# Moving spectral pieces between the borders of token pairs and the opened steps of a fused Fourier mixing and SiLU kernel

## The chip, the core and the metric

The kernel runs on one core of a Trainium2 chip. The metric is the device time of one execution in microseconds (us). The time before is the median of three runs.

The core's engines work side by side, each through its own instructions in order: PE multiplies matrices and writes to PSUM, a small memory of eight banks; DVE and ACT are the vector and the scalar engine, and both read PSUM; POOL is the third general engine and also issues transfers; SP issues transfers only. A wait on one engine holds all that stands behind it on that engine.

## What is computed

Eight sequences of 3008 tokens with 256 channels are filtered in the frequency domain, and every token then passes through a two-layer network with a SiLU between. All in fp32.

```python
X = np.fft.rfft(x, axis=1)
F = (filt_r + 1j * filt_i)[None, :, :]
y = np.fft.irfft(X * F, n=x.shape[1], axis=1)
...
x = y.reshape(B * S, D)
h = x @ w_in
g = h * (1.0 / (1.0 + np.exp(-h)))
return (g @ w_out).astype(np.float32)
```

## The kernel before

**The token network sets the beat.** The tokens of a sequence are handled in six *token pairs* (two blocks of 256, 256 or 240 tokens, with a fast 2x2 scheme that needs seven products instead of eight). A pair takes eight *steps*, one for each double column block of the weights. A step issues seven full-array matmuls of `hidden` (into the PSUM banks `x` and `yz`) and, between them, seven of `project` for the step before (into the four accumulator banks `a0` to `a3`). A pair ends with its last `project`, which runs between the `hidden` matmuls of the next pair's first step; then `drain` copies the four banks out, and they are free until the next step's `project` opens the new pair's sums. I call that moment, the end of a pair's first step, the *border*. Eight sequences of 48 steps make 384 steps, and their order on each engine is written out by hand: `put(step, rnd, piece)` places a piece of other work behind round `rnd` (0 to 7) of a step.

**The Fourier filter of the next sequence runs in between.** While the network works on sequence b-1, the pieces for sequence b are put among its 48 steps. I number these steps as *places* 0 to 47; the code counts them from the sequence's own start, `at`, so `at - 40` is place 8 of the sequence before, `at + 12` is place 12 of the sequence itself, and `at - 64` is place 32 two sequences ahead. Borders lie at the end of places 0, 8, 16, 24, 32 and 40. For sequences 2 to 7 (sequence 1 has an older form, sequence 0 a prologue) the pieces are:

- *folded stage 1* (`fold`, `stage1_fold`, `evict_fold`, `pairs_fold`), three times (f = 0, 1, 2): DVE folds eight rows of x, PE multiplies into four banks `pf`, ACT copies two of them out, DVE combines these with the other two, and POOL stores eight pieces to DRAM (`d1`);
- *stage 1 of the two middle groups* (`stage1` 6 and 7, `pairs_t1`), banks `pa`;
- *forward* (`forward_two`, g = 0, 2, 4): PE multiplies loaded rows (`load_t2`) into four banks `pb`; `free_two` has ACT copy two of them to SBUF; DVE multiplies all four by the filter (`multiply_two`, four calls of two operations, 128x512 each) and adds (`add_two`);
- *inverse* (`inverse_two`, g = 0, 2, 4): PE fills four banks `pc`; ACT copies two out (`even_two`), DVE combines (`rows_two`, `ends_two`), POOL stores to DRAM (`d2`);
- *last stage* (`stage3`, g = 0 to 7): PE fills two banks `pd` from loaded rows (`load_t4`), and `evict_y` copies one by DVE and one by ACT into the network's input `y`. `stage3` 6 and 7 of a sequence run while the network already works on it.

PE reaches these pieces as blocks of small matmuls (32x32 or 64x64 corners of the array, many side by side).

**Two ways to find banks.** All eight banks are in use in a normal step. At a border the accumulators `a0`..`a3` are free besides the two spare banks `f`, and also `x` and `yz` once the step's last sums are taken: `join` puts `stage3` there, and a step in `joined` starts the new pair with the products for `a0` and `a1`, so that `a2` and `a3` have longer. Elsewhere a step is *opened* (`open_step`, the set `opened`): its first two `project` matmuls run first, then the piece uses `x` and `yz` (`HIDDEN`) and `f`, and only then `hidden` begins.

The places before, for one sequence's pieces within the 48 steps of the network:

```
border  0: stage1_fold 1, stage3 4        opened  4: stage1 6, 7
border  8: stage1_fold 2, stage3 5        opened 12: forward 0
border 16: inverse 0, stage3 7 and 6      opened 20: forward 2
border 24: inverse 2                      opened 28: forward 4
border 32: inverse 4                      opened 38: stage3 0, 1
border 40: stage1_fold 0 (of the next), stage3 3 and 2
```

Lines that the prediction names: L936 (`hidden` matmuls, tiles `px` and `pyz`), L999 (`project` matmuls, `acc`), L907 (`combine`, all of DVE's sums of the network and the token sums `ty` of `tokens`, which stand at places 6, 11, 22, 26, 38 and 46), L508 (`pf`), L564 (`pb`), L602 (`pc`), L740 (`pd`), L576 (`uc`, the copies of `free_two`), L608 (`q`, the copies of `even_two`), L614 (`rows_two`), L619 and L620 (`ends_two`), L584 (`multiply_two`), L589 and L590 (`add_two`), L499 (`fold`), L444 and L445 (`pairs_fold`), L533 (`load_t2`), L717 (`load_t4`), L1017 and L1019 (`drain`).

Of the kernel before, what the change touches and what calls it, by code (L numbers as in the profile page):

```python
# [53 lines left out]
B, S, C = 8, 3008, 256  # L54
# [173 lines left out]
def kernel(  # L228
# [88 lines left out]
    def bank(b, name, spare=None):  # L317


        if early[0] is None and spare in ("x", "yz"):  # L320
            return xps.tile([128, 2, C], FP32, name=name, tag=spare)
        if early[0] is None and spare is not None:
            return accps.tile([128, 2, C], FP32, name=name, tag=f"a{spare}")
        if early[0] is None:
            return fps.tile([128, 2, C], FP32, name=name, tag="f")
        early[0] += 1
        k = early[0] % 8
        if k < 2:
            return fps.tile([128, 2, C], FP32, name=name, tag="f")
        if k > 5:  # L330
            return xps.tile([128, 2, C], FP32, name=name, tag="x" if k == 6 else "yz")
        return accps.tile([128, 2, C], FP32, name=name, tag=f"a{k - 2}")

    def spectral(b):
# [166 lines left out]
        def stage1_fold(f):  # L501
            ut = us.pop("f")
            rhs = x_all[:, 0, 0], x_all[:, 1, 0], ut[:, 0], ut[:, 1]
            ps = [bank(b, f"pf_{b}_{f}_{q}", (0, 1, None, None)[q]) for q in range(4)]
            for k in range(4):
                for q in range(4):
                    rows = slice(32 * q, 32 * q + 24)
                    nc.tensor.matmul(out=ps[q][32 * k:32 * k + 32], lhsT=wq_t[rows, k], rhs=rhs[k][rows],  # L508
                                     start=True, stop=True)
            us["ps"] = ps  # L510
# [42 lines left out]
            prods[g] = []  # L553

        def forward_two(g):
            ps = {(k, ri): bank(b, f"pb_{b}_{g}_{k}_{ri}", HIDDEN[ri] if k else None)
                  for k in range(2) for ri in range(2)}
            for a in range(2):
                for j in range(4):
                    for k in range(2):  # L560
                        par, at = slot_source(k, j)
                        for ri in range(2):
                            rows = slice(64 * par + 32 * ri, 64 * par + 32 * ri + 32)
                            nc.tensor.matmul(out=ps[k, ri][32 * j:32 * j + 32, a, :],  # L564
                                             lhsT=dn_t[rows, 4 * (g + a) + at, :],
                                             rhs=t2s[g + a][rows, at, :], start=True, stop=True)
# [212 lines left out]
    def plan(b, part):  # L779
# [3 lines left out]
        if b == 1:  # L783
            for u in range(2, 8):
                put(at + u - 49, 3, part["stage1"], u)
        else:
            put(at - 72, 0, part["reverse_x"])
            for f, step, load, places in ((0, -56, -66, ((-60, 3), (-60, 5), (-59, 5), (-58, 5))),
                                          (1, -48, -55, ((-52, 3), (-52, 5), (-51, 5), (-50, 5))),
                                          (2, -40, -44, ((-42, 5), (-41, 3), (-41, 5), (-40, 3)))):  # L790
                put(at + load, 0, part["load_fold"], f)
                for k, (fold_step, rnd) in enumerate(places):
                    put(at + fold_step, rnd, part["fold"], f, k)

# [9 lines left out]
            put(at - 44, 5, part["pairs_t1"], 1)  # L804
        put(at - 38, 0, part["load_t2"], 0)
        put(at - 38, 0, part["load_t2"], 1)
        if b > 1:
            return plan_two(b, part)
        for g, places in enumerate((
# [25 lines left out]
        join(at - 8, part, 2, 3)  # L835
        plan_rest(b, part)

    def plan_two(b, part):

        at = STEPS * b  # L840
        for g, step in ((0, -36), (2, -28), (4, -20)):
            open_step(at + step, (part["forward_two"], g), (part["free_two"], g))
            for after, rnd, piece, *args in ((0, 3, "multiply_two", 0, 0), (0, 5, "multiply_two", 0, 1),
                                             (1, 3, "add_two", 0), (1, 5, "multiply_two", 1, 0),
                                             (2, 3, "multiply_two", 1, 1), (3, 3, "add_two", 1)):
                put(at + step + after, rnd, part[piece], g, *args)
            put(at + step + 4, 7, part["inverse_two"], g)
            joined.add(at + step + 4)
            for i in range(2):
                put(at + step + 4, 7, part["even_two"], g, i)  # L850
            for after, rnd, piece, i in ((5, 5, "rows_two", 0), (6, 3, "rows_two", 1),
                                         (6, 5, "ends_two", 0), (7, 3, "ends_two", 1)):
                put(at + step + after, rnd, part[piece], g, i)
        put(at - 12, 1, part["load_t4"], 0)
        put(at - 12, 1, part["load_t4"], 1)
        open_step(at - 10, *alone(part, 0), (part["stage3"], 1))
        put(at - 10, 3, part["evict_y"], 1, 0)
        put(at - 10, 5, part["evict_y"], 1, 1)
        join(at - 8, part, 2, 3)
        plan_rest(b, part)  # L860

    def open_step(step, *pieces):

# [560 lines left out]
```

## Time and profile before

| | |
|---|---|
| median of three runs | 2594.2 us (2593.73 to 2595.83) |
| profiled execution, own time | 2589.6 us |
| its span (first to last instruction) | 2587.8 us |
| granted TensorE clock, mean | 0.997 |
| PE busy | 2538.9 us, 98% of the span |
| DVE busy | 1668.8 us, 64% |
| ACT busy | 1104.0 us, 43% |
| POOL busy | 442.7 us, 17% |
| `project` matmuls, L999 `acc` | 5376 records, 1508.9 us busy, 375 ns each |
| `hidden` matmuls, L936, four groups | 5376 records |

How to read it. An fp32 matmul stands in the trace as two records, so a network matmul is "x2". Records overlap: one lasts some 375 ns, and the next starts after 216 ns. What a matmul costs the stream is therefore the distance from its start to the next start, not its duration. In the timeline each row has its start, its length, the engine, the source line, the operation with the tile written and the tiles read, its shape, and how many records were merged; a bracket is idle time in front of it with what ended it. Most of the shares are means over 48 places that repeat for each sequence, and what follows is read place by place in the 48 steps from 1029.5 to 1344.3 us, in which the network works on sequence 3 and the filter on sequence 4.

### The profile page before, as it was taken

How to read it: one execution, taken by the hardware profiler on the slowest of the kernel's cores; microseconds unless marked ns; L12 is line 12 of the kernel's file. 1: busy time of each engine (PE TensorE's matmuls, PEld its weight loads, DVE VectorE, ACT ScalarE, POOL GpSimd, SP SyncE). 2: the span in 40 equal slices, each digit the busy share in tenths (PEclk: the TensorE clock that was granted, in tenths of full speed). 3: DMA queues.
4: the chain of work that ended last, by engine and by line, in shares of the span. 5: the costliest groups of instructions: out<-in, count | busy, mean ns of one | idle time of the engine just before them, and what ended most of it. 6: DMA issues, size and time to landing. Idle time of an engine off the chain costs nothing.

```text
span 2587.8 us, 47087 instructions
## 1 busy us (share of the span) xinstructions
PE 2538.9 (98%) x18810; PEld 2177.6 (84%) x18810; DVE 1668.8 (64%) x3451; ACT 1104.0 (43%) x3039; POOL 442.7 (17%) x682
## 2 busy tenths in 40 slices
PE   8999999999999999999999999999999999999998
PEld 6688888888888888888888888888888888888987
DVE  7866666676666666767666676666666666545544
ACT  3544444444444444444444444444444444444443
POOL 3212111211121111311122111211121112101101
PEclk9999999999999999999999999999999999999999
DMA  9522232231222312323223211331132311200000
GB/s 294 155 60 68 68 77 63 64 90 46 58 70 58 98 44 52 73 65 88 50 61 80 74 56 50 84 84 54 49 75 68 75 42 33 62 15 15 16 9 16
DMA packets 122739, 171.83 MB, mean 66 GB/s; under 512 B 20500, under 2 KB 96244, under 8 KB 121636
## 3 DMA queue, kind: packets, MB, share of 16 engines
q1 hardware_dynamic: 97352, 117.88, 17.4%
q0 software_dynamic: 22320, 45.80, 6.7%
q10 hardware_dynamic: 2848, 5.15, 0.7%
q8 instruction: 147, 2.41, 0.4%
q14 instruction: 72, 0.59, 0.1%
HBM read 96.91 MB, written 81.26 MB: 69 GB/s over the span
## 4 chain that ended last, share of the span: by engine, by line
PE 94%; DMA 3%; DVE 1%; ACT 1%; issue 0%; SPq 0%; POOL 0%; ACTq 0%; POOLq 0%; DVEq 0%
PE acc L999 43%; PE px L936 25%; PE pyz L936 19%; PE pd L740 3%; PE pb L564 1%; PE pc L602 1%; PE pf L508 1%; DMA filt<-in_filt_i_dram 0%; PE pa L420 0%; DMA w_t<-in_x_dram 0%; DVE g L907 0%; ACT uc L576 0%; DMA d<-q 0%; DMA w_t<-d 0%; DMA t<-d 0%
## 5 line engine op out<-in xcount | busy, mean ns | idle before, releaser
L999 PE MATMUL acc<-g,w_t 128*128 128x256 f32 (+1 forms) x5376 | 1508.9, 375 | 0.4 <-DVE g L907 0.4
L999 PEld LDWEIGHTS acc<-g,w_t 128*128 128x128 f32 x5376 | 1021.1, 190 | 120.1 <-ACT q L608 4.8
L907 DVE TENSOR_TENSOR g<-pyz,abc 128x256 f32<-128x256 f32 (+1 forms) x1152 | 480.0, 417 | 636.0 <-ACT abc L957 312.4
L907 DVE TENSOR_TENSOR g<-g 128x256 f32<-128x256 f32 (+3 forms) x1152 | 598.6, 520 | 196.8 <-ACT g L940 183.6
L936 PE MATMUL px<-ty,w_t 128*128 128x256 f32 (+1 forms) x2304 | 677.3, 376 | 1.5 <-ACT abc L951 1.1
L940 ACT ACTIVATE g<-g 128x256 f32<-128x256 f32 (+1 forms) x1152 | 472.9, 411 | 251.8 <-DVE g L907 251.8
L907 POOL TENSOR_TENSOR s<-s 128x256 f32<-128x256 f32 (+1 forms) x331 | 260.4, 804 | 1636.2 <-DVE s L1017 1473.8
L936 PEld LDWEIGHTS px<-ty,w_t 128*128 128x128 f32 x2304 | 434.0, 190 | 59.9 <-ACT abc L951 4.0
L936 PE MATMUL pyz<-y,w_t 128*128 128x256 f32 (+1 forms) x1536 | 455.9, 379 | 7.4 <-DVE g L907 6.9
L936 PEld LDWEIGHTS pyz<-y,w_t 128*128 128x128 f32 x1536 | 282.9, 190 | 57.6 <-DVE g L907 17.0
L951 ACT COPY abc<-px 128x256 f32<-128x256 f32 (+1 forms) x384 | 141.5, 369 | 373.1 <-PE px L936 373.1
L957 ACT COPY abc<-px 128x256 f32<-128x256 f32 (+1 forms) x384 | 141.8, 369 | 321.8 <-PE px L936 321.6
L940 ACT ACTIVATE g<-px 128x256 f32<-128x256 f32 (+1 forms) x384 | 146.1, 381 | 299.8 <-PE px L936 299.8
L936 PE MATMUL px<-y,w_t 128*128 128x256 f32 (+1 forms) x768 | 234.0, 386 | 13.2 <-ACT uc L576 12.5
L936 PE MATMUL pyz<-ty,w_t 128*128 128x256 f32 (+1 forms) x768 | 225.9, 376 | 0.3 <-DVE g L907 0.2
L936 PEld LDWEIGHTS px<-y,w_t 128*128 128x128 f32 x768 | 139.6, 190 | 49.0 <-ACT uc L576 21.1
L936 PEld LDWEIGHTS pyz<-ty,w_t 128*128 128x128 f32 x768 | 143.9, 190 | 20.3 <-DVE g L907 1.5
L944 ACT COPY abc<-px 128x256 f32<-128x256 f32 (+1 forms) x384 | 136.1, 354 | 50.9 <-PE px L936 50.9
L1017 ACT COPY s<-acc 128x512 f32<-128x512 f32 (+1 forms) x94 | 54.3, 578 | 47.5 <-issue 28.5
L740 PEld LDWEIGHTS pd<-wn_t,t 48*64 48x64 f32 x3072 | 49.1, 135 | 21.2 <-ACT g L940 15.9
L623 POOL DMA_DIRECT2D d<-low x36 | 22.1, 615 | 214.2 <-DVE low L619 214.2
L740 PE MATMUL pd<-wn_t,t 48*64 48x47 f32 x3072 | 53.5, 232 | 2.4 <-issue 2.1
(157 smaller groups left out, 1335.3 us busy)
## 6 DMA issues: line engine op xcount, KB each, us to landing
t<-d SPq DMA_DIRECT2D x120, 192.0 KB
t<-d SPq DMA_DIRECT2D x84, 256.0 KB
out_dram<-s SPq DMA_DIRECT2D x64, 256.0 KB
d<-q POOLq DMA_DIRECT2D x48, 256.0 KB, 5.2
d<-low POOLq DMA_DIRECT2D x36, 256.0 KB, 4.2
xr<-in_x_dram SPq DMA_DIRECT2D x6, 1472.0 KB
out_dram<-s SPq DMA_DIRECT2D x30, 240.0 KB
x_all<-in_x_dram SPq DMA_DIRECT2D x72, 96.0 KB
```

The lines of the kernel that those rows point to most:

```text
L508: nc.tensor.matmul(out=ps[q][32 * k:32 * k + 32], lhsT=wq_t[rows, k], rhs=rhs[k][rows], start=True, stop=True)
L564: nc.tensor.matmul(out=ps[k, ri][32 * j:32 * j + 32, a, :], lhsT=dn_t[rows, 4 * (g + a) + at, :], rhs=t2s[g + a][rows, at, :], start=True, ...
L602: nc.tensor.matmul(out=ps[j][cols, ri, :], lhsT=en_t[rows, g + a, k, ri, :], rhs=zs[k, ri][0][rows, a, :], start=True, stop=True)
L740: nc.tensor.matmul(out=ps[h][c0:c0 + 64, cb, 3 - i if back else i, :], lhsT=t4[rows, i, 128 * cb + c0:128 * cb + c0 + 64], rhs=table[rows, ...
L907: eng.tensor_tensor(out=out, in0=in0, in1=in1, op=op)
L936: nc.tensor.matmul(out=out, lhsT=w_t[:, jp, c, 0], rhs=rhs, start=start, stop=True, skip_group_check=True)
L940: nc.scalar.activation(out=g[:, k, 0:n], in_=g[:, k, 0:n] if src is None else src, func=AFT.Silu)
L944: nc.scalar.copy(out=sums[:, 0, 0:n], in_=xo)
L951: nc.scalar.copy(out=sums[:, 1, 0:n], in_=xo)
L957: nc.scalar.copy(out=sums[:, 2, 0:n], in_=xo)
L999: nc.tensor.matmul(out=acc[pair][i][:, h, 0:n], lhsT=w_t[:, jp, c, 1], rhs=g[:, k, 0:n], start=(jp == 0 and h == 0), stop=last, skip_group ...
L1017: copy(out=s[:, 2 * i:2 * i + 2, 0:n], in_=acc[pair][i][:, :, 0:n])
```

## The change

Nothing is added or taken away: every engine has the same instructions (PE 9292 rows of the program, DVE, ACT, POOL and SP likewise) in another order, some in other banks. After the change the places are:

```
border  0: stage1_fold 2, stage3 4        opened  4: stage1 6, 7
border  8: forward 0, stage3 5            opened 12: stage3 6, 7
border 16: inverse 0, forward 2
border 24: inverse 2, forward 4
border 32: inverse 4, stage1_fold 0 (of the next)
border 40: stage1_fold 1 (of the next), stage3 3 and 2      opened 38: stage3 0, 1
```

The steps behind borders 16, 24 and 32 are put into `opened` too, without a piece of their own: there two `project` matmuls run before `hidden` begins. `forward_two` for g = 2, 4 writes its four banks to `a2`, `a3` and `x`, `yz`; for g = 0 to `f`, `f` and `a0`, `a1`. `stage1_fold` 0 uses `x`, `yz`, `a2`, `a3`. The products, sums and folds on DVE, the loads and the reversed copy of x (`reverse_x`) move along.

```diff
         def stage1_fold(f):
...
-            ps = [bank(b, f"pf_{b}_{f}_{q}", (0, 1, None, None)[q]) for q in range(4)]
+            home = (*HIDDEN, *ACCS) if f == 0 else (0, 1, None, None)
+            ps = [bank(b, f"pf_{b}_{f}_{q}", home[q]) for q in range(4)]
...
         def forward_two(g):
-            ps = {(k, ri): bank(b, f"pb_{b}_{g}_{k}_{ri}", HIDDEN[ri] if k else None)
+            home = ((None, None), (0, 1)) if g == 0 else (ACCS, HIDDEN)
+            ps = {(k, ri): bank(b, f"pb_{b}_{g}_{k}_{ri}", home[k][ri])
                   for k in range(2) for ri in range(2)}
...
-            put(at - 72, 0, part["reverse_x"])
-            for f, step, load, places in ((0, -56, -66, ((-60, 3), (-60, 5), (-59, 5), (-58, 5))),
-                                          (1, -48, -55, ((-52, 3), (-52, 5), (-51, 5), (-50, 5))),
-                                          (2, -40, -44, ((-42, 5), (-41, 3), (-41, 5), (-40, 3)))):
+            put(at - 80, 0, part["reverse_x"])
+            for f, step, load, places, ends in (
+                    (0, -64, -73, ((-68, 3), (-68, 5), (-67, 5), (-66, 5)), ((1, 0), (1, 3))),
+                    (1, -56, -63, ((-60, 3), (-60, 5), (-59, 5), (-58, 5)), ((1, 3), (1, 5))),
+                    (2, -48, -55, ((-52, 3), (-52, 5), (-51, 5), (-50, 5)), ((1, 3), (1, 5)))):
...
-                put(at + step + 1, 3, part["pairs_fold"], f, 0)
-                put(at + step + 1, 5, part["pairs_fold"], f, 1)
+                for q, (after, rnd) in enumerate(ends):
+                    put(at + step + after, rnd, part["pairs_fold"], f, q)
+            opened.add(at - 63)
...
     def plan_two(b, part):
...
-        for g, step in ((0, -36), (2, -28), (4, -20)):
-            open_step(at + step, (part["forward_two"], g), (part["free_two"], g))
...
+        put(at - 42, 0, part["load_t2"], 0)
+        put(at - 42, 0, part["load_t2"], 1)
+        for g, step, places in (
+                (0, -40, ((-39, 3), (-39, 5), (-38, 3), (-38, 5), (-37, 3), (-36, 3))),
+                (2, -32, ((-31, 0), (-31, 2), (-29, 5), (-28, 3), (-28, 5), (-27, 3))),
+                (4, -24, ((-23, 0), (-23, 2), (-22, 2), (-21, 5), (-20, 2), (-18, 3)))):
+            if g:
+                plan_inverse(at + step, part, g - 2)
+                opened.add(at + step + 1)
+            put(at + step, 7, part["forward_two"], g)
+            put(at + step, 7, part["free_two"], g)
+            pieces = (("multiply_two", 0, 0), ("multiply_two", 0, 1), ("add_two", 0),
+                      ("multiply_two", 1, 0), ("multiply_two", 1, 1), ("add_two", 1))
+            for (place, rnd), (piece, *args) in zip(places, pieces):
+                put(at + place, rnd, part[piece], g, *args)
+        plan_inverse(at - 16, part, 4)
...
+    def plan_inverse(step, part, g):
+
+        put(step, 7, part["inverse_two"], g)
+        joined.add(step)
+        for i in range(2):
+            put(step, 7, part["even_two"], g, i)
+        for after, rnd, piece, i in ((1, 5, "rows_two", 0), (2, 3, "rows_two", 1),
+                                     (2, 5, "ends_two", 0), (3, 3, "ends_two", 1)):
+            put(step + after, rnd, part[piece], g, i)
...
+    def two_alone(step, part, g):
+
+        open_step(step, *alone(part, g), (part["stage3"], g + 1))
+        put(step, 3, part["evict_y"], g + 1, 0)
+        put(step, 5, part["evict_y"], g + 1, 1)
...
-            join(at + 16, part, *((7,) if b == B - 1 else (6, 7)))
+                join(at + 16, part, 7)
+            else:
+                two_alone(at + 12, part, 6)
```

`load_t2` 0 and 1 stood at `at - 38` before, and `inverse_two` four steps behind each forward at the same borders as now.

More of the change, by code (lines that the diff above doesn't have):

```diff
@@ L804, in plan @@
             put(at - 44, 5, part["pairs_t1"], 1)
+            return plan_two(b, part)
         put(at - 38, 0, part["load_t2"], 0)
         put(at - 38, 0, part["load_t2"], 1)
[L807 to L808 removed]
         for g, places in enumerate((
@@ L836, in plan @@
         plan_rest(b, part)
+    def plan_inverse(step, part, g):
[6 more added lines that the diff above has]
+            put(step + after, rnd, part[piece], g, i)
     def plan_two(b, part):
         at = STEPS * b
-        for g, step in ((0, -36), (2, -28), (4, -20)):
-            open_step(at + step, (part["forward_two"], g), (part["free_two"], g))
[L843 to L853, printed above, removed]
@@ L854, in plan_two @@
+        plan_inverse(at - 16, part, 4)
         put(at - 12, 1, part["load_t4"], 0)
         put(at - 12, 1, part["load_t4"], 1)
-        open_step(at - 10, *alone(part, 0), (part["stage3"], 1))
-        put(at - 10, 3, part["evict_y"], 1, 0)
-        put(at - 10, 5, part["evict_y"], 1, 1)
+        two_alone(at - 10, part, 0)
         join(at - 8, part, 2, 3)
         plan_rest(b, part)
+    def two_alone(step, part, g):
+        open_step(step, *alone(part, g), (part["stage3"], g + 1))
+        put(step, 3, part["evict_y"], g + 1, 0)
+        put(step, 5, part["evict_y"], g + 1, 1)
```

## The prediction

> **What bounds the kernel.** First the chain of work that ended last, then what PE waited for from 397 to 2285 us (sequences 1 to 6 in the network), then the timeline of PE, place by place.
>
> ```profile
> PE 94%; DMA 3%; DVE 1%; ACT 1%; issue 0%; SPq 0%; POOL 0%; ACTq 0%; POOLq 0%; DVEq 0%
> ```
> ```profile
> PE px L936 <- ACT uc L576: 12.5, 18, 0.8
> PE pyz L936 <- DVE g L907: 6.5, 6, 1.1
> PE pd L740 <- issue: 2.8, 4, 1.3
> PE pb L564 <- DMA t<-d: 1.0, 3, 0.7
> ```
>
> PE's stream is the time; only what stops or lengthens it counts. The waits sit at the added pieces: 18 times (three forwards, six sequences) `px` waits for `free_two`'s copy, six times `pyz` for DVE, four times a `pd` block finds no instruction, three times a forward's rows are late.
>
> ```profile
> 1194.42 0.59 PE L936 MATMUL pyz<-y,w_t 128*128 128x256 f32 x2
> 1194.94 1.49 PE L602 MATMUL pc<-z,e_t 32*32 32x256 f32 x64
> 1196.37 0.70 PE L936 MATMUL px<-y,w_t 128*128 128x256 f32 x2
> 1197.06 0.70 PE L999 MATMUL acc<-g,w_t 128*128 128x256 f32 x2
> ```
> ```profile
> 1088.28 0.66 PE L508 MATMUL pf<-x_all,wq_t 24*32 24x512 f32 x8
> ...
> 1089.35 1.16 PE L740 MATMUL pd<-wn_t,t 48*64 48x47 f32 x64
> 1090.44 0.70 PE L936 MATMUL px<-y,w_t 128*128 128x256 f32 x2
> ```
> ```profile
> 1210.93 0.70 PE L936 MATMUL pyz<-y,w_t 128*128 128x256 f32 x2 [1.08 <-DVE g L907]
> ...
> 1216.21 1.03 PE L999 MATMUL acc<-g,w_t 128*128 128x256 f32 x4
> 1217.17 1.49 PE L564 MATMUL pb<-t,d_t 32*32 32x256 f32 x64
> 1219.32 0.70 PE L936 MATMUL px<-y,w_t 128*128 128x256 f32 x2 [0.66 <-ACT uc L576]
> ```
> ```profile
> 1281.90 2.08 PE L740 MATMUL pd<-wn_t,t 48*64 48x47 f32 x128
> 1283.91 0.70 PE L936 MATMUL px<-y,w_t 128*128 128x256 f32 x2
> ```
>
> Border 24, border 8, opened 28, opened 38. A network matmul costs 0.43 (start to start); a step of fourteen, 6.04 (5.67 at 240 tokens). A block costs: `pc` 1.43 (1194.94 to 1196.37), `pf` 1.07, one `stage3` 1.09, two 2.01, `pb` 2.15, of which 0.66 is the copy's wait; free of it `pb` is 1.43, like `pc` with as many records of one length. Entering and leaving a block adds 0.2 (0.52 for 0.43 before `pc`; 0.10 in the `px` after it), and an opened step 0.06 in the next `pyz`.
>
> **The change, place by place.** Costs over the plain stream, for one sequence's 48 places, undisturbed:
>
> - Opened 12: forward 0, 2.8 (0.2 + 2.56 from the `pb` at 1109.67 to the `px` at 1112.23), becomes two `stage3`: 2.2, as at 38. **-0.6**.
> - Openings 20 and 28 go: 2.4 each (0.10 + 2.15 + 0.10 + 0.06). **-4.8**.
> - Border 16: `pc` and two `stage3`, 3.6 (0.2 + 1.43 + 2.01), becomes `pc` + `pb`: 0.2 + 0.06 + 1.43 + 1.43 = 3.1. **-0.5**.
> - Border 24: 1.9 (1.43 + 0.2, and 0.26 in the first `acc`, which waits for `even_two`'s copy of a0) becomes 3.1. **+1.2**.
> - Border 32: 1.9 becomes 0.2 + 0.06 + 1.43 + 1.07 = 2.75. **+0.9**.
> - Border 8: `pf` becomes `pb`. **+0.35**.
> - 0, 4, 38, 40 keep their blocks.
>
> Sum without DVE: -3.45. What hides the rest: at 16 and 24 the two `q` copies (1.07 for the pair) run under the 1.43 of `pb`, so a0 and a1 are empty when it ends; the two `uc` copies (1.07) run under the two `project` matmuls put first (0.97). `px` then finds its bank with 0.2 to spare. Uncovered, that is the old 0.66 each. At 32 four copies (2.1) run under `pf` and two matmuls (2.1): even, within 0.1.
>
> **DVE** is the price. An operation on 512 columns takes 0.684, two in a row 1.40, a fold on 1024 1.22, a token sum `ty` 1.5; the network's own work is 2.87 of 6.04. It has two gaps in a step, of 1.65 before `g2` (the sum of L907 that waits for `yo`) and 1.4 after: two pairs fit, no third. Place 26 has three groups already:
>
> ```profile
> 1205.62 1.40 DVE L614 TENSOR_TENSOR q<-q,pc 128x512 f32<-128x512 f32 x2
> 1207.27 0.42 DVE L907 TENSOR_TENSOR g<-pyz,abc 128x256 f32<-128x256 f32 x1 [0.24 <-ACT abc L957]
> 1207.61 0.68 DVE L619 TENSOR_TENSOR low<-q 128x512 f32<-128x512 f32 x1
> ...
> 1208.93 0.69 DVE L907 TENSOR_TENSOR ty<-y 128x512 f32<-128x512 f32 x1
> ...
> 1210.46 0.42 DVE L907 TENSOR_TENSOR g<-pyz,abc 128x256 f32<-128x256 f32 x1
> ```
>
> The last sum reads `yz`, which the next `pyz` overwrites: that is the 1.08 idle in the third fence, 1.25 against the stream. After the change `add_two` (1.40) stands ahead of `q`. The queue from 1205.62: 1.40 + 1.40, then `g2` at 1208.3 for 1207.27, so everything behind is 1.0 later: the last `hidden` matmul of the step, which adds onto what `g2` reads, by some 0.35, ACT's SiLUs behind the sums, and the next `pyz` by the whole, 2.25 for 1.25. **+1.0** at 26 (all gap filled: 1.4; none: 0). Place 28 gets `multiply_two` 1.40 and a fold 1.22 before `g2`, 1.0 over the gap less 0.1, then another fold: last sum 0.55 late, of which the normal slack takes 0.19. With the restart 0.1, **+0.5** (0 to 0.9). Places 17, 25 and 33 get products or `pairs_fold` at once after the block; the PE blocks give DVE 2.5 to 2.9 idle there (it stood idle 1.65 at 25 already), and I count six operations, 4.2, into 5.4 of step plus that: 0, at most 0.5 each. Places 9 to 12 hold two pairs: 0.
>
> Per sequence **-3.45 + 1.5 = -1.95**, times six: **-11.7**.
>
> **Once**, while sequence 0 is in the network: sequence 1's old form is not in `joined` at border 32, so the opened step's first `project` writes a2, which holds `pf`. It must wait for two q copies, the `x` copy and two DVE operations after `pc`: 1.91 of block, then 3.1 of queue, against 1.07 of `pf`: +2.1 (0 to 3). Its adds at 28 to 30 meet the folds: DVE 7.0, 7.0, 5.9 a step: +2.5 (1 to 4). Together **+4.6**.
>
> **Queues.** SP's loads are moved with their waits. `load_t2` 0 and 1 (four issues, 2.68) started at 1103.41 after the last fold's stores and the `pb` at 1109.67 still met them; by the starts of the steps that forward cost 2.7 to 6.4, over six sequences 3.4 more than the 2.8 above. Now the last stores are stage 1's, at place 5, with the load at 6 and the forward at the end of 8: some 13 us earlier relative to need. **-3.4** (0 to -3.4). `stage3` 7's load (two issues, 1.33) now stands behind four of `load_t2` at border 8: 4.0 of issue and at most 6.3 to land, 10 of the 19 us until opened 12. `reverse_x` blocks SP's later loads by 29 us in one wait at most; its readers still have seven places, 42 us. POOL gets eight stores (0.5 each) at place 33 ahead of the inverse's; those wait for DVE until 35 anyway. If that cover failed, `load_t4` would be late for opened 38.
>
> **Instruction waits**: the 2.8 of `pd <- issue` fell on 192 records in a row (border 16) and on 160 (40). The new blocks are of 128, and 128 in a row at 38 never waited. **-2.5** of it (0 to -2.8).
>
> Sum: -11.7 + 4.6 - 3.4 - 2.5 = **-13** against the profiled execution's 2589.6, which is 4.6 under the median 2594.2. The median has these irregular waits too, so I take -13 there: **2581**.
>
> The Trainium skill, "TensorE: Matmul & The Clock Gate" (The HAM clock gate), speaks against longer standstills: the clock halves after an idle window of about 3.4 us, which runs freely. The rows here: after the late forward (four waits within 792.87 to 796.50) matmuls came 0.85 apart instead of 0.43 for some 3 us, costing 1.7; after 1.25 at place 27 they did not. By the rule the 2.25 that I expect there stays below a window, and the sum stands; if a window happened to catch it, the clock rival's price would be due. "TensorEngine Tiling (Array Packing)" (Key Properties) lets the array drain only when the tiling changes; `pc` to `pb` keeps it, but no row shows that pair. By it each such junction would cost less than my 1.43 leaves, an estimate of 2 us in all.
>
> **Rivals.**
>
> *More gain.* DVE's gaps absorb the additions at 26 and 28: 2581 - 1.5 x 6 = 2572. For it: DVE is 64% busy. Against: place 26 already stops PE.
>
> *The clock drops* behind the longer wait at 27: 1.7 x 6 = 10, time 2591, within 0.2%. For it: 792 to 800 us. Against: the block there took 4.49 (792.01 to 796.50) for 1.43, 3.1 lost, more than 2.25.
>
> *DVE at the borders decides (slower).* At 17, 25 and 33 products hold a2 and a3 and delay the sums that free `yz`. If DVE is one pair late there, 1.4 less 0.19, it costs 3 x 1.2 x 6 = 22: 2603. It turns to a loss once added stalls pass 13 / 6 = 2.2 per sequence. For it: three operation pairs in one step fit only by PE's block. Against: before, DVE idled there.
>
> *Not what it says*: the PE rows are the same in number, and the order of the built program has the two openings gone; nothing is left of this one.
>
> **Chances.** Forecast 2573 to 2588, 0.59; more gain 0.10; clock 0.14; DVE at the borders 0.17. Beyond 0.2% (5 us, about what this kernel's measurement tells from none) faster means under 2589: 0.59 + 0.10 + 0.03 of the clock case = 0.72. Same 0.13, slower 0.15 (of the border case, 0.02 ends as same). Range 2570 to 2593: up to the clock case, down to the larger gain.
>
> **What would show it.** Right: no `uc` wait in PE's list (12.5 gone), a `pyz` wait for DVE of some 2 at place 27, `pc` and `pb` together 2.9, `pd <- issue` near 0, a wait of `acc` for DVE near 305 us. Wrong: `acc` waiting for DVE at 16, 24 or 32 in every sequence, `px` still waiting for `uc` or `tf`, or starts 0.85 apart behind place 27.

## The result, and the profile after

The changed kernel takes 2573.24 us (median of four runs, 2568.37 to 2574.01) against 2593.97 for the kernel before beside it (2593.33 to 2595.83, four runs): ratio 0.9915, 95% interval 0.9898 to 0.9932. A later set gave 2572.48 and 0.9926 (0.9910 to 0.9943). The forecast was 2581, the range 2570 to 2593. One run of e4 below (10792 us, granted clock 0.581) and one of e5 (2642 us, 0.947) were slow ones and stand outside the ratios.

The profiled execution took 2574.0 (span 2571.5, granted clock 0.996), 15.6 less than the one shown of before. From the first `hidden` matmul to the end it went from 2513.9 to 2496.0, which is 17.9 less; that first matmul came at 75.5 us for 73.9, and the time outside the span grew by 0.7.

Lines of the source have moved: `hidden` is L957 (was L936), `project` L1020, DVE's sums L928, `pb` L566, `pc` L604, `pf` L509, `pd` L742, `add_two` L591 and L592, `rows_two` L616, `ends_two` L621 and L622. First the chain of work that ended last, as shares of the span by engine, then PE's waits from 380 to 2285 us (sequences 1 to 6 in the network: us in all, times, longest).

```profile
PE 93%; DVE 3%; DMA 3%; ACT 1%; issue 0%; SPq 0%; ACTq 0%; POOL 0%; POOLq 0%; DVEq 0%
```
```profile
PE pyz L957 <- DVE g L928: 9.7, 6, 1.6
PE pd L742 <- issue: 1.0, 2, 0.6
PE pd L742 <- DVE g L928: 0.3, 1, 0.3
```

The 18 waits for the copy `uc` (12.5) and the three for late rows are gone, and DVE's share of the chain has gone from 1% to 3%: in each of the six sequences the chain passes through DVE once, from place 25 to 27, for 9.7 us where it was 3.5. Next the timeline of PE while sequence 3 is in the network: border 16, border 8, opened 12.

```profile
1138.26 0.57 PE L957 MATMUL pyz<-y,w_t 128*128 128x240 f32 x2
1138.75 1.50 PE L604 MATMUL pc<-z,e_t 32*32 32x256 f32 x64
1139.89 1.65 PE L566 MATMUL pb<-t,d_t 32*32 32x256 f32 x64
1141.47 1.08 PE L1020 MATMUL acc<-g,w_t 128*128 128x240 f32 x4
1142.38 0.57 PE L957 MATMUL px<-y,w_t 128*128 128x240 f32 x2
```
```profile
1085.16 0.59 PE L957 MATMUL pyz<-y,w_t 128*128 128x256 f32 x2
1085.68 1.50 PE L566 MATMUL pb<-t,d_t 32*32 32x256 f32 x64
1087.11 1.15 PE L742 MATMUL pd<-wn_t,t 48*64 48x47 f32 x64
1088.19 0.70 PE L957 MATMUL px<-y,w_t 128*128 128x256 f32 x2
```
```profile
1106.42 1.03 PE L1020 MATMUL acc<-g,w_t 128*128 128x256 f32 x4
1107.38 2.08 PE L742 MATMUL pd<-wn_t,t 48*64 48x47 f32 x128
1109.39 0.70 PE L957 MATMUL px<-y,w_t 128*128 128x256 f32 x2
```

No row has a bracket. `pb` alone starts 1.43 before `pd`, as forecast; but from `pc` to `pb` it is only 1.14 (1138.75 to 1139.89), and the pair up to what follows takes 2.72 (to 1141.47) for the 2.86 forecast. Now place 27, where the one wait is left: PE, then DVE from the additions of forward 4 on.

```profile
1202.09 0.70 PE L957 MATMUL pyz<-y,w_t 128*128 128x256 f32 x2
1202.63 0.59 PE L957 MATMUL px<-y,w_t 128*128 128x256 f32 x2
1203.06 0.59 PE L1020 MATMUL acc<-g,w_t 128*128 128x256 f32 x2
1205.27 0.70 PE L957 MATMUL pyz<-y,w_t 128*128 128x256 f32 x2 [1.62 <-DVE g L928]
```
```profile
1199.10 0.68 DVE L591 TENSOR_TENSOR z<-z,p 128x512 f32<-128x512 f32 x1
1199.70 0.68 DVE L592 TENSOR_TENSOR z<-z,p 128x512 f32<-128x512 f32 x1
1200.30 1.40 DVE L616 TENSOR_TENSOR q<-q,pc 128x512 f32<-128x512 f32 x2
1201.62 0.42 DVE L928 TENSOR_TENSOR g<-pyz,abc 128x256 f32<-128x256 f32 x1
1201.95 0.68 DVE L621 TENSOR_TENSOR low<-q 128x512 f32<-128x512 f32 x1
1202.67 0.69 DVE L622 TENSOR_TENSOR q<-q 128x512 f32<-128x512 f32 x1
...
1204.80 0.42 DVE L928 TENSOR_TENSOR g<-pyz,abc 128x256 f32<-128x256 f32 x1
```

DVE has no idle time from the additions to the sum at 1204.80, which frees `yz` for the `pyz` at 1205.27. The matmul behind it starts 0.54 later, at full rate.

**Place by place.** A place's cost is the distance from its first `hidden` matmul to the next place's, less fourteen network matmuls. The second column has the terms of the prediction's sum; the third was the same within 0.02 in sequences 1 to 5, waits for instructions apart. Six folds are placed at border 32, the first with sequence 0 in the network and none with sequence 6, so "six sequences" counts one there.

| | forecast | measured |
|---|---|---|
| border 8 | +0.35 | 2.35 to 2.69: +0.34 |
| opened 12 (without late rows) | -0.6 | 2.20 after, as forecast |
| border 16 | -0.5 | 3.81 to 3.12: -0.69 |
| opening 20 | -2.4 | -2.46 |
| border 24 | +1.2 | 1.69 to 2.71: +1.02 |
| places 26 to 29 (opening 28, DVE) | -2.4 + 1.0 + 0.5 = -0.9 | 3.74 to 2.65: -1.09 |
| border 32 | +0.9 | 1.87 to 2.72: +0.85 |
| **one sequence** | **-1.95** | **-2.63** |
| six sequences | -11.7 | -15.8 |
| once, sequence 0 in the network | +4.6 | +5.3 (its 48 steps +6.6, less the usual 0.85 of border 32 and 0.44 of places 28 and 29) |
| late rows | -3.4 | -3.6 |
| waits for instructions | -2.5 | 4.9 to 1.55: -3.4 |
| sum | -13 | -17.5, of the -17.9 from the first `hidden` to the end |

Two rows need a word. The measured column takes the -0.6 of opened 12 over from the forecast, because the kernel before shows the forward there only with its late rows: 20.4 over the six sequences before and 13.2 after, 7.2 less, which leaves 3.6 for the late rows. By e7 below the split is another, -0.2 a sequence and -6.0 for the rows. And 0.7 of the 4.9 stands just behind the block of border 16 of sequence 5, where the profile names ACT's `y`; it comes at the same record of PE's stream at which e8 shows a wait for instructions.

### The profile page after: what moved, and what is told of

Same layout as the page of the kernel before. It is cut to its first block, busy times and chain, and to the rows that moved or that the text cites. A ratio compares the mean times of both kernels' runs of the same rounds, so it can differ in the third digit from the quotient of the medians.

```text
span 2571.5 us, 47151 instructions
## 1 busy us (share of the span) xinstructions
PE 2531.8 (98%) x18810; PEld 2183.9 (85%) x18810; DVE 1660.8 (65%) x3451; ACT 1103.6 (43%) x3039; POOL 438.5 (17%) x682
## 3 DMA queue, kind: packets, MB, share of 16 engines
q8 instruction: 147, 2.41, 0.4%
## 4 chain that ended last, share of the span: by engine, by line
PE 93%; DVE 3%; DMA 3%; ACT 1%; issue 0%; SPq 0%; ACTq 0%; POOL 0%; POOLq 0%; DVEq 0%
PE acc L1020 43%; PE px L957 25%; PE pyz L957 19%; PE pd L742 3%; PE pc L604 1%; PE pb L566 1%; DVE g L928 1%; PE pf L509 1%; DVE q L616 1%; PE pa L420 0%; DMA filt<-in_filt_i_dram 0%; DMA w_t<-in_x_dram 0%; DMA d<-q 0%; DMA w_t<-d 0%; DVE ty L928 0%
## 5 line engine op out<-in xcount | busy, mean ns | idle before, releaser
L1020 PE MATMUL acc<-g,w_t 128*128 128x256 f32 (+1 forms) x5376 | 1509.2, 375 | 2.8 <-DVE tf L445 2.4
L1020 PEld LDWEIGHTS acc<-g,w_t 128*128 128x128 f32 x5376 | 1020.6, 190 | 128.0 <-ACT q L610 9.5
L928 DVE TENSOR_TENSOR g<-pyz,abc 128x256 f32<-128x256 f32 (+1 forms) x1152 | 479.4, 416 | 612.0 <-ACT abc L978 335.9
L928 DVE TENSOR_TENSOR g<-g 128x256 f32<-128x256 f32 (+3 forms) x1152 | 592.9, 515 | 196.7 <-ACT g L961 183.6
L957 PE MATMUL px<-ty,w_t 128*128 128x256 f32 (+1 forms) x2304 | 678.0, 376 | 1.1 <-ACT abc L972 0.6
L928 POOL TENSOR_TENSOR s<-s 128x256 f32<-128x256 f32 (+1 forms) x331 | 256.1, 791 | 1654.5 <-DVE s L1038 1434.9
L957 PEld LDWEIGHTS px<-ty,w_t 128*128 128x128 f32 x2304 | 434.1, 190 | 59.9 <-ACT abc L972 3.9
L957 PE MATMUL pyz<-y,w_t 128*128 128x256 f32 (+1 forms) x1536 | 456.1, 379 | 10.9 <-DVE g L928 10.3
L957 PEld LDWEIGHTS pyz<-y,w_t 128*128 128x128 f32 x1536 | 282.0, 190 | 65.1 <-DVE g L928 26.6
L957 PE MATMUL px<-y,w_t 128*128 128x256 f32 (+1 forms) x768 | 231.3, 383 | 0.7 <-DVE y L756 0.7
L957 PE MATMUL pyz<-ty,w_t 128*128 128x256 f32 (+1 forms) x768 | 225.8, 376 | 0.2 <-DVE g L928 0.2
L957 PEld LDWEIGHTS px<-y,w_t 128*128 128x128 f32 x768 | 142.1, 190 | 25.4 <-ACT t L427 4.9
L957 PEld LDWEIGHTS pyz<-ty,w_t 128*128 128x128 f32 x768 | 143.3, 190 | 20.2 <-DVE g L928 1.0
L742 PEld LDWEIGHTS pd<-wn_t,t 48*64 48x64 f32 x3072 | 48.5, 135 | 16.6 <-ACT g L961 11.7
L742 PE MATMUL pd<-wn_t,t 48*64 48x47 f32 x3072 | 52.8, 232 | 1.2 <-issue 1.0
```

Of the source, the lines that this page charges most:

```text
L742: nc.tensor.matmul(out=ps[h][c0:c0 + 64, cb, 3 - i if back else i, :], lhsT=t4[rows, i, 128 * cb + c0:128 * cb + c0 + 64], rhs=table[rows, ...
L928: eng.tensor_tensor(out=out, in0=in0, in1=in1, op=op)
L957: nc.tensor.matmul(out=out, lhsT=w_t[:, jp, c, 0], rhs=rhs, start=start, stop=True, skip_group_check=True)
L1020: nc.tensor.matmul(out=acc[pair][i][:, h, 0:n], lhsT=w_t[:, jp, c, 1], rhs=g[:, k, 0:n], start=(jp == 0 and h == 0), stop=last, skip_group ...
```

## The experiments

The medians of before beside them were 2591.61 (e1 to e4), 2590.45 (e5 to e8) and 2592.26 (e9 to e11); beside e12 it took 2590.16, one run.

### e1: the kernel before once more

> The kernel before once more, unchanged, to see what of its time is irregular. In the first profile the forward of g = 0 (opened 12) cost 2.7 to 6.4 us over the stream in the six sequences, and border 16 had 2.8 us of waits for instructions. Theory (irregular waits): in this execution the same two places vary again, in other sequences and by other amounts, the other places keep their cost within 0.1 us, and the difference of the two executions' times is the difference of these waits. Rival (fixed waits): the same waits in the same sequences, within 0.3 us, and the 4.6 us by which the first profiled execution was under the median come from somewhere else.

It took 2595.36. The late rows and the waits for instructions came in the same sequences and at the same places (border 16 of sequences 1, 3, 6; place 40 of 2, 4; forward 0 worst in sequence 2), the waits for instructions up to 0.6 larger or smaller and that forward 1.75 dearer. Of the 5.8 by which its span is longer than that of the execution shown, 4.6 lie before the network: the first `hidden` matmul came at 78.5 for 73.9. So the first theory fell: these waits are fixed in place, though not in size as the rival had it, and most of the difference between these two executions is the start.

### e2: sequence 1's border joined

```diff
-                joined.add(at + step)
+            joined.add(at + step)
```

> The changed kernel with sequence 1's border 32 (while sequence 0 is in the network) put into joined as well, so that the opened step's first two project matmuls go to a0 and a1 and a2 has time until its products are read. Theory: the 2.41 us wait of acc for DVE's tf at 310 us goes, and with it the slow clock behind it (matmuls 0.85 apart until 313.8 us, 1.6 us): 48 steps of sequence 0 shorter by 3.5 to 4.2 us, everything else as in the changed kernel, ratio to before 0.990. Rival (the clock drops anyway because pc and pf leave the array mostly idle): the wait goes but matmuls are still 0.85 apart, gain 2.0 to 2.5. Second rival (a0 and a1 are as late as a2, since the x copy stands between): gain under 1.

2568.39 (2566.08 to 2571.17), ratio 0.9911 (0.9897 to 0.9925). Border 32 with sequence 0 in the network: in the changed kernel PE's timeline has

```profile
306.80 0.66 PE L509 MATMUL pf<-x_all,wq_t 24*32 24x512 f32 x8
...
310.45 2.05 PE L1020 MATMUL acc<-g,w_t 128*128 128x256 f32 x4 [2.41 <-DVE tf L445]
312.29 1.06 PE L957 MATMUL px<-y,w_t 128*128 128x256 f32 x2
313.14 0.84 PE L957 MATMUL pyz<-y,w_t 128*128 128x256 f32 x2
313.82 0.59 PE L1020 MATMUL acc<-g,w_t 128*128 128x256 f32 x2
```

and in busy time by stretches (PE, weight loads, DVE, ACT, POOL, then the granted clock as a share of full speed, DMA)

```profile
306.00:310.00 4.00, 2.04 (x65) 0.72 (x48) 1.66 (x3) 2.15 (x4) 3.84 (x5) 1.00 0.19 59
310.00:312.00 2.00, 1.55 (x4) 1.31 (x5) 0.30 (x1) 0.00 (x0) 0.16 (x1) 0.55 0.77 176
312.00:314.00 2.00, 2.00 (x7) 1.61 (x6) 0.00 (x0) 0.37 (x1) 0.00 (x0) 0.60 0.57 107
314.00:316.00 2.00, 2.00 (x11) 1.67 (x11) 1.84 (x5) 0.69 (x2) 0.00 (x0) 1.00 0.00 0
```

The first `project` waits 2.41 for DVE to have read `a2`, and then the clock is 0.55 and 0.60 for 3.4 us: four matmuls take 3.37 (310.45 to 313.82) where four take 1.73, 1.64 lost. With the border joined the same place reads

```profile
305.27 0.66 PE L509 MATMUL pf<-x_all,wq_t 24*32 24x512 f32 x8
...
306.45 1.13 PE L1020 MATMUL acc<-g,w_t 128*128 128x256 f32 x4
307.42 0.68 PE L957 MATMUL px<-y,w_t 128*128 128x256 f32 x2
```

Wait and slow matmuls are gone together: places 32 and 33 fell from 7.30 to 3.42, 3.9 as the theory had it, and the 48 steps of that sequence from 330.2 to 324.4 (the rest at places 0 and 1, which also differ by 1.4 between two executions of the changed kernel). So the border's cost was 2.41 + 1.64 and not the 2.1 of the prediction. The ratio by itself does not tell this kernel from the changed one (0.9911 and 0.9915, with overlapping intervals); the gain is read from the traces.

### e3: the token sums of place 26 moved away

```diff
-    combines = ((-2, 1), (6, 1), (11, 5), (22, 5), (26, 6), (38, 1))
+    combines = ((-2, 1), (6, 1), (11, 5), (22, 5), (31, 3), (38, 1))
```

> The changed kernel with the token sum ty of place 26 moved to round 3 of place 31, where DVE has 2.87 us of its own in 6.04. It tells whether DVE's queue at place 26 is what PE waits for behind it. Theory: two pairs too many stay (add_two and rows_two before g2, ends_two behind it): the last sum of place 26 is 1.0 late instead of 2.6, the wait of pyz at place 27 falls from 1.62 to about 0.4, places 26 to 28 cost 0.9 instead of 2.2 in each of six sequences; 1.3 x 6 = 8 us faster than the changed kernel, about 2565. Place 31 adds nothing (0 to 0.2). Rival (the wait comes from ACT or from project's banks): place 27 stays within 0.3 us.

2561.21 (2560.25 to 2567.88), ratio 0.9891 (0.9875 to 0.9906). Place 27 went from 1.88 to 0.36 in every sequence, 9.1 over six, and place 26 kept its 0.33. So the wait at 27 is DVE's order in that step, 1.5 for one group of 1.5.

### e4: the step behind a border not opened

```diff
-            opened.add(at - 63)
...
-                opened.add(at + step + 1)
```

> The changed kernel without opening the steps behind borders 16, 24 and 32: hidden's px follows the block at once, as at the other borders. It tells what the two project matmuls in front hide. Theory: px waits for the copies of free_two and evict_fold again, 0.66 at 17 and 25 and 0.7 to 0.9 at 33; 0.06 is saved in each opened step; 1.9 to 2.2 a sequence, 11 to 13 us slower than the changed kernel, about 2585. At sequence 0's border 32 the wait of acc for tf becomes a wait of px and pyz for their copies, shorter than 2.41. Rival (the copies are done in time, opening is idle): within 2 us of the changed kernel.

2585.64, ratio 0.9971 (0.9959 to 0.9982), and 2.2 a sequence over the changed kernel. PE's waits over the whole span:

```profile
PE px L955 <- ACT uc L578: 7.9, 12, 0.7
PE px L955 <- ACT tf L516: 4.5, 6, 0.9
```

Twelve waits behind `pb` at borders 16 and 24, six behind `pf` at 32: exactly the covers that the prediction named, two `project` matmuls put first, and 0.66 and 0.75 each without them. By the ratios two thirds of what the change brought (0.0056 of 0.0085) hang on these two lines; by the traces it is half of what the six sequences gained (12.3 of 24.3). At sequence 1's border the opening is what does harm: without it places 32 and 33 cost 5.29 for 7.30.

### e6: only the token sums moved, in the kernel before

```diff
-    combines = ((-2, 1), (6, 1), (11, 5), (22, 5), (26, 6), (38, 1))
+    combines = ((-2, 1), (6, 1), (11, 5), (22, 5), (27, 5), (38, 1))
```

> The kernel before with one edit: the token sums of place 26 stand one step later. Theory (the wait of pyz at place 27 comes from the third group of DVE operations in one step, not from the total of DVE's work): the 1.28 at place 27 goes in all six sequences and at most 0.2 appears behind place 27, so 1.1 x 6 = 6.7 us faster than before, 2587. So a third of what the change brought was to be had by this alone. Rival (DVE is late by the total of its work there): the wait moves to place 28 with its size, 2594.

2581.07 (2579.67 to 2585.53), ratio 0.9957 (0.9942 to 0.9972). Place 27 fell from 4.45 to 3.11 in all six sequences, 8.0 in all, and nothing appeared behind it. (One place far from the edit differs from the kernel before, border 16 of sequence 3; see e12.) Not the total of DVE's work stops PE there but three groups in one step.

### e7: forward 0 one step later, in the kernel before

```diff
-            open_step(at + step, (part["forward_two"], g), (part["free_two"], g))
+            late = 0 if g else 1
+            open_step(at + step + late, (part["forward_two"], g), (part["free_two"], g))
...
-                put(at + step + after, rnd, part[piece], g, *args)
+                put(at + step + late + after, rnd, part[piece], g, *args)
```

> The kernel before with one edit: forward 0, with its products and sums, stands one step later (place 13), the loads of its rows where they were. Theory (the rows of forward 0 are late because their four loads stand behind the last fold's stores; one step of 6 us is more than they are late): the late rows' 3.5 us over six sequences go, and the halved clock behind the worst of them with it: 3.5 to 5.5 us faster, about 2589, and no wait of pb for DMA is in the list. Rival (the wait follows the opening wherever it stands, or the rows' loads are later than a step): no difference.

2585.31 (2583.14 to 2589.57), ratio 0.9978 (0.9967 to 0.9989): 5.1 faster. No wait of `pb` for DMA is left, and forward 0 costs 2.39 in every sequence (3.10 and -0.71). Over six sequences it had cost 20.4, so the late rows were 6.0 and an undisturbed forward 2.4: the 2.8 that the prediction took as undisturbed held 0.4 of lateness. Its two terms together (0.6 x 6 + 3.4 = 7.0) were right, 7.2 measured.

### e8 and e11: PE's stream moved by sixteen instructions

```diff
-    idle(27)
+    idle(43)
```

In the kernel before (e8) and in the changed kernel (e11).

> The kernel before with sixteen more idle matmuls at the start of PE's stream, and nothing else changed. Theory (the waits of pd for its instructions come at fixed places in PE's instruction stream, where a long run of small matmuls meets the edge of a stretch of instructions that is fetched): they leave sequences 1, 3 and 6 at border 16 and 2 and 4 at border 40 and turn up in other sequences or other blocks; the stretches of 48 steps are otherwise as long as before. Rival (they are set by what runs at those places: loads, DVE, the length of the run): they stay in the same sequences, sizes within 1 us.

> The changed kernel with sixteen more idle matmuls at the start of PE's stream, and nothing else changed. Theory (where PE finds no instruction is set by where a run of small matmuls stands in its stream, and the 2 us that the change saved of it are position luck as much as shorter blocks): the waits at place 11 of sequence 4 and at place 37 of sequence 3 go, others turn up elsewhere, in all between 0 and 4 us. Rival (runs of 128 in place of 192 and 160 all but end these waits): at most 0.5 in all.

In e8 (2590.71) the waits left border 16 of sequence 1 and place 40 of sequence 2, fell from 1.5 to 0.55 at border 16 of sequence 3, and came at border 16 of sequence 5 (0.9): in all 1.7 for 4.9. In e11 (2577.98) both old places were clean, and waits stood at place 8 of sequence 5 (0.55) and at place 40 of sequences 1, 3, 5 and 6 (0.3, 0.8, 0.8, 1.3): in all 3.8 for 1.55. The theory was right, and the records within the runs say it more sharply. At border 16 of sequence 3 PE stopped behind 183 small records before and behind 151 in e8: 32 earlier, which is what sixteen matmuls of two records move it. So the address is fixed to the record. And every such stop that the five traces show as idle time within a run of small records lies behind at least 124 of them: the addresses of place 40 (141 and 154 before) came to stand at 109 and 122 in e8, and cost nothing (sequence 2) or 0.2 (sequence 4). By this a run of 192 would expose some 70 records, one of 128 only its last four, an estimate from these few stops. That speaks for shorter runs as a cause, as the prediction said, but does not show it: moved by sixteen matmuls, the changed kernel waits longer (3.8) than the kernel before (1.7). Where an address falls in a run is luck, worth up to 1.5 a time here.

### e10: the changed kernel once more

> The changed kernel unchanged, for a second profile. Theory (the places' costs are fixed, the start before the network is what differs from one execution to the next): every place of sequences 1 to 6 costs what it did within 0.1, except blocks where PE waits for instructions (place 11 of sequence 4, 37 of sequence 3), which come again with another size; border 32 of the first sequence again costs 7.3 with the halved clock behind it; time 2568 to 2576, and its difference to the first profile is that of the first hidden matmul within 1 us. Rival (the halved clock behind border 32 is chance): border 32 costs 5.5 or less.

2572.48 (2572.08 to 2575.19). Every place of the six sequences came within 0.1; the instruction waits in the same two places (0.52 each for 0.75 and 0.69); border 32 of the first sequence again with its wait of 2.41, and this time the slow matmuls went on for 6.1 us, 3.1 lost for 1.64 (8.73 for 7.30 at places 32 and 33).

### e12: a longer wait without a block in front

```diff
-                (4, -24, ((-23, 0), (-23, 2), (-22, 2), (-21, 5), (-20, 2), (-18, 3)))):
+                (4, -24, ((-23, 0), (-23, 2), (-22, 2), (-22, 2), (-20, 2), (-18, 3)))):
```

> The changed kernel with one edit: two more DVE operations (one product pair of forward 4, 1.40 us) stand at place 26, ahead of the inverse's rows, instead of at place 27. The wait at place 27 grows from 1.6 to about 3.0, with no block of small matmuls in front of it; at border 32 of the first sequence a wait of 2.4 behind 3.0 of small matmuls was followed by matmuls at half the clock. Theory (what counts is the time since the last full-array matmul, 5.6 there, 4.5 at the late forward of the kernel before, so 3.4 here is too short): no half clock; place 27 costs 1.4 more, some of it comes back at 28: 6 to 9 us in all, about 2580. Rival (a standstill over 2.3 is enough): matmuls 0.85 apart behind the wait in most of the six sequences, 1.7 each more: about 2590. By the Trainium skill, "TensorE: Matmul & The Clock Gate" (The HAM clock gate), a window of 3.4 us without work is needed and the windows run freely, so a gap of 3.4 would catch one seldom or never.

2582.63 (one run, whose first `hidden` matmul came 2.1 later than in the changed kernel). The test missed its aim, for the wait did not grow; it came twice:

```profile
1207.23 0.70 PE L957 MATMUL pyz<-y,w_t 128*128 128x256 f32 x2 [1.27 <-DVE g L928]
1207.77 0.59 PE L957 MATMUL px<-y,w_t 128*128 128x256 f32 x2
1208.20 0.59 PE L1020 MATMUL acc<-g,w_t 128*128 128x256 f32 x2
1210.41 0.70 PE L957 MATMUL pyz<-y,w_t 128*128 128x256 f32 x2 [1.62 <-DVE g L928]
```

The extra pair makes `g2` late, which stops PE one matmul before the step's end (place 26: 0.33 to 1.53), and the wait at 27 stays as it was. So one more pair in a full step costs 1.2, 7.2 over six sequences, the price per pair that the rival "DVE at the borders" had. No half clock behind either wait. The theory on the clock, that the time since the last full-array matmul decides, fell without it. In the kernel before, at border 16 of sequence 3, 5.2 lie between two full-array matmuls (1.28 of them idle, the rest small matmuls), with the next ones at full rate:

```profile
1146.31 0.33 PE L740 MATMUL pd<-wn_t,t 48*64 48x47 f32 x9 [1.28 <-issue]
1146.58 0.67 PE L936 MATMUL px<-y,w_t 128*128 128x240 f32 x2
1147.09 0.57 PE L999 MATMUL acc<-g,w_t 128*128 128x240 f32 x2
```

The same border in e6, whose edit lies ten places further on, reads

```profile
1145.84 0.34 PE L740 MATMUL pd<-wn_t,t 48*64 48x47 f32 x9 [1.25 <-issue]
1146.11 1.17 PE L936 MATMUL px<-y,w_t 128*128 128x240 f32 x2
1147.07 1.01 PE L999 MATMUL acc<-g,w_t 128*128 128x240 f32 x2
```

with a granted clock of 0.50 from 1147 to 1149 us, and place 17 costs 1.66 more. So the standstill is the same in both and the clock is not.

### e5 and e9: what the other runs point to

```diff
-                joined.add(at + step)
+            joined.add(at + step)
...
-                (4, -24, ((-23, 0), (-23, 2), (-22, 2), (-21, 5), (-20, 2), (-18, 3)))):
+                (4, -24, ((-23, 0), (-23, 2), (-21, 5), (-20, 3), (-20, 5), (-19, 3)))):
...
-    combines = ((-2, 1), (6, 1), (11, 5), (22, 5), (26, 6), (38, 1))
+    combines = ((-2, 1), (6, 1), (11, 5), (22, 5), (29, 5), (38, 1))
```

Besides, the folds of place 28 stand two steps later, at (-66, 3), (-66, 5), (-65, 3), (-65, 5), those of sequence 2, beside the older form, partly one step earlier, and the token sums of the first sequence stay at place 26.

> The changed kernel with three edits together: sequence 1's inverse is joined at border 32 too; the token sums of place 26 stand one behind the other DVE operations of place 29; and the additions and products of forward 4 and the folds behind it are spread so that no step holds more than two pairs of DVE operations beyond the network's own. Theory (DVE's order at places 26 to 31 and sequence 1's border are all that the change gave back): the 2.65 us that places 26 to 28 cost over the plain stream in each of the six undisturbed sequences fall to some 0.2, 14.5 us in all; border 32 of the first sequence gives 3.9 as before, its places 28 to 31 another 1.3: about 2553, and no wait of pyz for DVE is left. Rival (the last step's gain of 9.1 from moving the sums alone is all there is, the added 0.5 at place 28 is the opened step and not DVE): 2573 - 9 - 4 = 2560, with place 28 still at 0.4 or more.

> The kernel of e5_best unchanged, for a profile at the full clock. Theory: places 26 to 31 of the six undisturbed sequences cost at most 0.3 together over the plain stream, border 32 of the first sequence as in e2_joined (4.2 and -0.7), its places 28 to 31 at most 1.3 where the changed kernel has 2.8; no wait of pyz for DVE longer than 0.5. Time 2550 to 2554. Rival: 0.4 or more is left at place 28 in every sequence.

2551.64 against 2590.45, ratio 0.9844 (0.9831 to 0.9858), and 2550.57 in the second run, whose trace is used. Places 26 to 31 cost 0.01 over the plain stream in each of the six sequences, border 32 of the first sequence 3.42 with 33, places 28 to 31 there 1.2. PE's waits for sequences 1 to 6:

```profile
PE px L959 <- issue: 0.4, 1, 0.4
PE pd L742 <- issue: 0.4, 1, 0.4
PE pd L742 <- DVE g L930: 0.3, 1, 0.3
```

So DVE's order and sequence 1's border are what the change gave back, 21.9 us of it (2572.48 of e10 to 2550.57, one run beside it), and this version beats both kernels. Almost all that is left above the plain stream in these sequences is the blocks themselves.

## Why the prediction was right

**The sign and the mechanism** were right: the blocks at the borders need no copy to be waited for (e4 takes the cover away and gets the waits back at the price named), DVE pays for it at places 26 to 29 (e3 and e9 take the wait away), and little else stops PE (1.0 for instructions and 0.3 for DVE in six sequences). The forecast lines are there: no `uc` wait, one `pyz` wait for DVE at place 27, little waiting for instructions, an `acc` wait for DVE at 310 us (305 forecast).

**Too small a gain per sequence** (-1.95 for -2.63, the -0.6 of opened 12 taken as forecast in both). The step that failed is "free of it `pb` is 1.43, like `pc`", used for two such blocks in a row. Behind `pc` the next block starts after 1.14, and the pair takes 2.72: some 0.15 less at each of borders 16 and 24, and 0.05 of the opened step on top. This is the point where "TensorEngine Tiling (Array Packing)" (Key Properties) of the Trainium skill was weighed: by its rule that only a change of tiling drains the array, the estimate was 2 us in all; the measured 0.14 (2.86 to 2.72) at twelve borders is 1.7. The rows agree with the rule as far as they go: 1.14 from `pc` to `pb`, which have one tiling, and 1.43 from `pb` to `pd` and, before, from `pc` to `pd`, which have two; that a drain is what makes the difference no run shows. The prediction left the 2 us out of the sum. The rest of the difference is DVE's, 0.2 at places 26 to 29.

**Forward 0** was mis-sized in two terms that offset each other. An undisturbed forward 0 cost 2.4 and not 2.8 (e7), so opened 12 gave -0.2 a sequence for -0.6, and its late rows gave -6.0 for -3.4. Together that is 7.2 for the 7.0 forecast, which is luck. By this split a sequence gained 2.2.

**Waits for instructions** came out near the forecast (-3.4 for -2.5) by luck as well: e8 and e11 show that they depend on where an address falls.

**DVE at 26 and 28** was right in kind and nearly in size. `g2` is late and costs 0.33 at place 26 (the 0.35 forecast), the last sum stops the next `pyz` (1.88 at place 27, 1.62 of it as a wait), and the folds cost 0.44 at 28 and 29 for 0.5. Together 2.65 for the 2.85 that 0.1 + 2.25 + 0.5 gave.

**Once**: the price of sequence 1's border was mis-sized, +2.1 for some 4. The wait itself was 2.41. The step that failed is that the clock was given its rival at place 27 and none here: 1.64 were lost to it in one execution, 3.1 in another. The adds were 2.5 in the forecast, at places 28 to 30, and 1.57, at 29 to 31.

**Rivals.** More gain (2572) hit the number by other causes: the additions at 26 and 28 were not absorbed. The clock did not drop behind place 27. DVE at the borders did not come: no `acc` waits for DVE at borders 16, 24 or 32 of sequences 1 to 6.

**The offset.** The step "the median has these irregular waits too, so I take -13 there" failed: the waits are fixed in place (e1, e8). The profiled execution lay 4.6 under the median, and 1.9 to 4.6 of that is its early start: the first `hidden` matmul came at 73.9 there and at 75.8 to 78.5 in the four other executions of this kernel or of it with a small edit. Against the 2595.36 of e1 the change is 21, like the 20.7 of the medians; 3.0 of it is e1's later start (78.5 for 75.5), and 19.1 lie behind the first `hidden` matmul. So the network gained 18 to 20 for the 13 forecast (the two profiles of each kernel taken crosswise), and the rest of the 20.7 is within what the start varies by. Why the start differs so much from one execution to the next was not looked into.

## What to carry to other kernels

When the matrix engine's stream is the time, add up each place's distance from start to start against the plain stream; waits in brackets show only part of it. Moving blocks to where banks are free pays when two other products can go in front of the matmul that needs the copied bank, and the price then turns up on the vector engine: count operation groups per step against its gaps, since each group too many costs its whole length less the slack, in every period. Look at the one odd period (the first sequence here) by itself: its one border cost 7.3 where an ordinary one costs 2.7.

## What the hardware showed

- **Half clock behind a standstill, in some executions.** Behind 3.0 of small matmuls and a wait of 2.41, at border 32 of the first sequence, the granted clock fell to 0.50 in all five executions that have this wait (changed kernel, e10, e3, e11, e12), for 3.4 us in one and 6.1 in another. Behind the waits of 1.62 at place 27 it never fell, nor behind two waits of 2.9 together within 5.0, with three full-array matmuls among them (e12). Between these the same place gave both: border 16 of sequence 3 with a wait of 1.28 in the kernel before (clock 1.00) and of 1.25 in e6 (0.50); forward 0 of sequence 2 with waits of 1.8 in the kernel before (0.50) and of 2.0 in e8 (1.00). So neither the length of the standstill nor the time since the last full matmul alone decides. That the windows of the prediction's clock rule run freely, and catch one such stretch and miss the next, would fit; it was not tested. By "TensorE: Matmul & The Clock Gate" (The HAM clock gate) of the Trainium skill an idle window of some 3.4 us is needed; here less idle time was enough when small matmuls lay around it.
- **Waits for instructions have addresses.** Sixteen matmuls more at the start moved them by 32 records, and those that stand as idle time within a run of small matmuls came behind 124 or more records in a row: 4.9 became 1.7 us in one kernel, 1.55 became 3.8 in the other. A difference of 2 or 3 us between two versions of this kernel can be that alone.
- **Two blocks of one tiling overlap.** `pb` starts 1.14 behind the start of `pc`, where `pd`, with another tiling, starts 1.43 behind it; the pair of `pc` and `pb` is 0.14 shorter than twice 1.43.
